# Loads of queries, keys, values and weight chunks in two or four transfers instead of one

## The chip, the core and the metric

The kernel runs on one core of a Trainium2 chip. The time is that of one launch in device microseconds (us); lower is better. The engines named below are PE (TensorE matmul), PEld (its weight load), DVE (VectorE), ACT (ScalarE), POOL (GpSimd) and SP (SyncE, which here only starts transfers). Transfers run on 16 DMA engines that all queues share.

## What is computed

Chunked softmax attention (8 batches, 8 heads, 576 rows, chunks of 64 rows) is followed by a mixture of eight experts with one expert per token. All 4608 tokens have 512 features.

```python
scores = scale * np.matmul(q_c, k_c.transpose(0, 1, 2, 4, 3))   # chunks of 64 x 64
attn = np.exp(scores - scores.max(-1, keepdims=True)); attn /= attn.sum(-1, keepdims=True) + 1e-09
x = np.matmul(attn, v_c)                                        # -> 4608 x 512
logits = x @ w_gate + modality_bias[modality_id]
e_idx = np.argmax(logits, axis=1)                               # gate_w: softmax weight of that expert
out[mask] = gate_w[mask, None] * (np.maximum(x[mask] @ w1[e], 0.0) @ w2[e])
```

## The kernel before

The attention goes in 18 rounds of 256 tokens. Round r needs one tile of queries and keys (`qk`, 128 partitions by 2048 numbers, 1024 KB) and one of values (`v`, 512 KB); three buffers each, so `load_qk(r + 3)` is called when the scores of round r are reduced, and `load_v(r + 3)` after the products with the values of round r. A round is `scores` (PE, L239), `differences` (DVE, L245 and L246), `exps` (ACT, L253), `halve` (POOL, L258), `transposes` (PE L291, copied by ACT L294), `values` (PE L306, copied by ACT L315), two `rows` (PE L324, DVE L326), `parts` (ACT L334) and `put`, which stores the round's 512 KB to DRAM (`xd`) from ACT's queue, L344. Round 0 has its own form, `opening` (L270), which computes heads 0 to 3 into one PSUM bank and heads 4 to 7 into another.

Rounds 0 to 7 run alone (the loop over `NPURE`). Rounds 8 to 17 are interleaved by `merge` with the experts' work: a `slot` is up to 384 tokens of one expert, gathered from `xd` by POOL (L756), and goes through eight chunks of 128 hidden features, each with 12 matmuls of `first` (L872) and up to 9 of `second` (L890). Chunks of weights are fetched in pairs (`fetch`, L819, 1024 KB, three buffers), split into two parts by ACT (`wh`, L830) and DVE (`wl`, L834). From slot 2 on a slot's tokens are also stored (`stash`) and read back in blocks (`place`). Thirteen slots run. After the eight pure rounds, `split` (PE L797, ACT L799, DVE L800) transposes the gathered tokens of slots 0 and 1. All orders are written out by hand; each engine runs its instructions in the order in which the program names them.

SP starts nearly all loads, in order. Round 9's queries and keys are loaded from ACT's queue instead (`load_qk(NPURE + 1, A)`, L1050), between the copies and the `parts` of round 7.

Each transfer that SP or ACT starts counts its landing on one of eight counters, DMAHW0 to DMAHW7, which are handed out in turn in the program's order of these transfers, those of both queues in one row. Before a transfer is started, its queue waits until the transfer that last had the same counter, the eighth before it, has landed. The queue's later instructions stand behind that wait: on ACT, its activations and copies too. POOL's transfers have counters of their own.

Of the kernel before, what the change touches and what calls it, by code (L numbers as in the profile page):

```python
# [18 lines left out]
B, H, S, D = 8, 8, 576, 64  # L19
P = 128  # L20
N = B * S
DM = H * D
# [46 lines left out]
NSPLIT = 2  # L69
# [26 lines left out]
def attention_moe(ctx: ExitStack, tc: tile.TileContext, qkv, mod, cst, bias, wcat, wfst, void, out):  # L96
    nc = tc.nc
    V, A, PE, G, SP = nc.vector, nc.scalar, nc.tensor, nc.gpsimd, nc.sync
# [14 lines left out]
    qks, vs, exs = {}, {}, {}  # L113
    st = {}

    def load_qk(r, eng=SP):
        if r < NT // 2 and r not in qks:
            qks[r] = ak.tile([P, 2, H, 2, 64], F32, name="qk", bufs=NB)
            eng.dma_start(qks[r].rearrange("p a h c s -> p (a h c s)"), qkv[r][:, 0:2 * 2 * DM])

    def load_v(r):
        if r < NT // 2:
            vs[r] = ak.tile([P, H, 2, D], F32, name="v", bufs=NB)
            SP.dma_start(vs[r].rearrange("p h c d -> p (h c d)"), qkv[r][:, 2 * 2 * DM:])

    cs = cp.tile([P, C_END], F32, name="cs")

    def consts(a, b):
        SP.dma_start(cs[:, a:b], cst[:, a:b])

    load_qk(0)
    consts(C_I, C_GW)
    load_qk(1)
    load_v(0)
    consts(C_GW, C_U)
    load_qk(2)
    load_v(1)
    consts(C_U, C_END)
    load_v(2)
    bs = cp.tile([P, 2, E], F32, name="bs")  # L140
    SP.dma_start(bs, bias)
# [668 lines left out]
    def expert(s):  # L810
        lv, k, _ = where(s)
        ereg[s] = SP.value_load(tabs[lv][0:1, k:k + 1], min_val=0, max_val=E - 1)

    def fetch(g, n=2):
        s, f = divmod(g, NF)
        if s not in ereg:
            expert(s)
        raw = rawr[g // 2 % 3][:, f % 2:f % 2 + n]
        SP.dma_start(raw, (wfst if s < NSPLIT else wcat)[ds(ereg[s], 1), :, f:f + n, :].rearrange("e p f c -> p (e f) c"))  # L819
        for i in range(n):  # L820
            raws[g + i] = raw[:, i]

# [24 lines left out]
    ereg = {}  # L847
# [62 lines left out]
    def slot(s):  # L910
# [5 lines left out]
        if s >= NSURE:  # L916
            expert(s)
            locate(s)
            for f in (0, 2, 4):
                fetch(s * NF + f)  # L920
            gather(s)
            stash(s)
            place(s)
            for f in range(AHEAD):
                wsplit(s * NF + f)
            for k in range(NK):
                turn(s, k)
                part(s, k)
        for f in range(NF):
            g = s * NF + f  # L930
            if s == 0:
                if f in FIRSTS:
                    fetch(FIRSTS[f])
            elif f % 2 == 0 and g + 6 < end:
                fetch(g + 6)
            h = first(xring[s % 2], W[g], g, nt * P)
            tick()
            if s < NSPLIT:
                advance((pooljobs,))
                advance((pooljobs,))  # L940
                wsplit(g + 2)
            else:
                advance()
                if s == NSPLIT and f == 0:
                    wsplit(g + 2)
                if g + AHEAD < end:
                    wsplit(g + AHEAD)
                advance()
            if pend is not None:
                second(ys, pend, W[g - 1], f - 1)  # L950
                tick()
            pend = h
            for c in PREP.get(s, REGULAR).get(f, ()) if s < NSURE else ():
                call(c, s if s > max(PREP) else 0)
            if s < NSPLIT:
                advance()
                advance()
            advance(pe=None if merging[0] else ts[1])
# [219 lines left out]
```

## Time and profile before

| | |
|---|---|
| runs | median 557.69 us of 3 (554.08 to 559.34) |
| profiled execution | 556.77 us by its own time, span 555.0 us |
| granted PE clock, mean | 0.989 |
| moved by DMA | 129.87 MB in 48626 packets, mean 234 GB/s |
| loads by SP | 17 of `qk`, 18 of `v`, 52 pairs of weight chunks; 1 of `qk` by ACT |

The profile page gives busy time and share of the span by engine; rows of the timeline read "start us, duration us, engine, line, operation, out<-in, count" and, in brackets, how long the engine had been idle and what ended it. ACTq and SPq are the instructions that these engines' sequencers handle themselves, here the starting of transfers. Rows of the windows view give busy time by engine in a stretch, then the granted clock, the DMA engines' busy share and GB/s. "us to landing" is the time from the start of a transfer's issue until it has landed; the profile has it for some transfers only.

### The profile page before, as it was taken

What the parts mean: (1) busy time and instruction counts of PE and PEld (TensorE: products, weight loads), DVE (VectorE), ACT (ScalarE), POOL (GpSimd) and SP (SyncE); (2) the same over time, 40 slices, a digit from 0 to 9 for tenths busy, and PEclk for the clock granted to TensorE, in tenths of its full rate; (3) what the DMA queues carried; (4) which work ended last, traced back from release to release, by engine and by line L of the source; (5) the groups of instructions that cost most, each with busy time, mean ns of one, the idle gap of its engine ahead of it and who ended that gap; (6) DMA issues with size and microseconds to landing.
All of it is one profiled execution on the core that took longest, in us unless ns stands there. A gap on an engine that the chain in (4) does not pass through costs nothing.

```text
span 555.0 us, 12219 instructions
## 1 busy us (share of the span) xinstructions
PE 525.4 (95%) x4933; PEld 474.2 (85%) x4933; DVE 359.5 (65%) x590; ACT 242.5 (44%) x403; POOL 163.9 (30%) x189
## 2 busy tenths in 40 slices
PE   7886997999999999999999999999999999999993
PEld 5875886988889899899999999999899999999992
DVE  4668786877686899656556465564656556466751
ACT  3453743555564443444434443443443434435530
POOL 3333455614356780340402205022040402202101
PEclk9999998999999999999999999999999999999997
DMA  8995897669766459597857668666685755557500
GB/s 341 411 363 190 303 410 271 220 209 411 272 235 196 155 153 351 201 309 213 276 175 230 243 209 254 194 217 199 224 280 163 267 165 205 192 188 237 184 20 27
DMA packets 48626, 129.87 MB, mean 234 GB/s; under 512 B 7100, under 2 KB 23852, under 8 KB 39600
## 3 DMA queue, kind: packets, MB, share of 16 engines
q1 hardware_dynamic: 36448, 99.34, 53.3%
q0 software_dynamic: 7072, 19.18, 9.9%
q10 hardware_dynamic: 5040, 10.49, 5.0%
q8 instruction: 40, 0.66, 0.5%
q14 instruction: 26, 0.21, 0.1%
HBM read 101.95 MB, written 27.83 MB: 234 GB/s over the span
## 4 chain that ended last, share of the span: by engine, by line
PE 72%; issue 14%; DVE 6%; DMA 3%; POOL 2%; ACT 1%; ACTq 0%; SPq 0%; POOLq 0%; DVEq 0%
PE y L872 26%; PE sb L890 20%; PE t L890 10%; PE y L324 5%; PE t L872 3%; PE y L306 2%; PE y L239 2%; PE t L291 1%; DMA xg<-xd,tk 1%; DMA qk<-in_qkv 1%; PE t L306 1%; PE sb L239 1%; POOL out L905 1%; DVE xr L326 1%; PE y L291 1%
## 5 line engine op out<-in xcount | busy, mean ns | idle before, releaser
L834 DVE TENSOR_TENSOR wl<-raw,wh 128x1024 fp32r<-128x1024 f32 x104 | 128.0, 1232 | 36.8 <-ACT wh L830 36.7
L880 ACT ACTIVATE hh<-y 128x384 fp32r<-128x384 f32 (+1 forms) x92 | 43.6, 474 | 179.6 <-PE y L872 179.4
L872 PE MATMUL y<-xh,wl 128*128 128x384 f32 (+1 forms) x368 | 120.7, 328 | 0.0
L872 PE MATMUL y<-xh,wh 128*128 128x384 f32 (+1 forms) x368 | 120.5, 327 | 0.0
L872 PE MATMUL y<-xl,wh 128*128 128x384 f32 (+1 forms) x368 | 120.1, 326 | 0.0
L881 DVE SCALAR_TENSOR_TENSOR hl<-y,hh 128x384 fp32r<-128x384 f32 (+1 forms) x92 | 49.1, 534 | 100.7 <-ACT hh L880 100.6
L830 ACT CAST wh<-raw 128x1024 fp32r<-128x1024 f32 x104 | 108.4, 1043 | 0.9 <-DMA raw<-in_wcat 0.9
L905 POOL DMA_INDIRECT out<-yo,tk x37 | 38.6, 1044 | 231.9 <-DVE yo L904 203.8
L890 PE MATMUL sb<-wh,hh 128*128 128x512 f32 x208 | 82.7, 397 | 0.0
L890 PE MATMUL sb<-wl,hh 128*128 128x512 f32 x208 | 81.9, 394 | 0.0
L890 PE MATMUL sb<-wh,hl 128*128 128x512 f32 x208 | 81.0, 389 | 0.0
L872 PEld LDWEIGHTS y<-xh,wh 128*128 128x128 f32 x368 | 69.2, 188 | 3.5
L872 PEld LDWEIGHTS y<-xl,wh 128*128 128x128 f32 x368 | 69.1, 188 | 3.2
L872 PEld LDWEIGHTS y<-xh,wl 128*128 128x128 f32 x368 | 69.1, 188 | 0.0
L756 POOL DMA_INDIRECT xg<-xd,tk x37 | 41.8, 1130 | 16.9 <-issue 8.7
L890 PEld LDWEIGHTS sb<-wh,hl 128*128 128x128 f32 x208 | 39.0, 188 | 8.8
L890 PEld LDWEIGHTS sb<-wh,hh 128*128 128x128 f32 x208 | 39.0, 188 | 6.2 <-issue 0.5
L540 POOL DMA_INDIRECT tab<-tg,pi x36 | 37.9, 1053 | 19.0 <-issue 13.3
L890 PEld LDWEIGHTS sb<-wl,hh 128*128 128x128 f32 x208 | 39.1, 188 | 4.5
L324 PE MATMUL y<-cs,xt 128*128 128x144 f32 x288 | 41.8, 293 | 1.1 <-DVE ex L246 0.8
L324 PEld LDWEIGHTS y<-cs,xt 128*128 128x128 f32 x288 | 38.5, 193 | 3.1 <-DVE ex L246 1.2
L258 POOL TENSOR_TENSOR sr<-ex 128x512 f32<-128x512 f32 x17 | 22.5, 1322 | 53.8 <-ACT ex L253 53.7
(234 smaller groups left out, 711.1 us busy)
## 6 DMA issues: line engine op xcount, KB each, us to landing
raw<-in_wcat SPq DMA_DIRECT2D x44, 1024.0 KB, 5.6
qk<-in_qkv SPq DMA_DIRECT2D x17, 1024.0 KB, 8.0
v<-in_qkv SPq DMA_DIRECT2D x18, 512.0 KB, 8.7
xd<-xr ACTq DMA_DIRECT2D x18, 512.0 KB, 5.2
raw<-in_wfst SPq DMA_DIRECT2D x8, 1024.0 KB, 4.9
xs<-xg SPq DMA_DIRECT2D x9, 768.0 KB, 7.7
xq<-xs SPq DMA_DIRECT2D x36, 192.0 KB, 3.8
qk<-in_qkv ACTq DMA_DIRECT2D x1, 1024.0 KB
```

Of the source, the lines that this page charges most:

```text
L239: PE.matmul(sp[c * 64:c * 64 + 64, u, h, :], b[us, 0, h, c], b[us, 1, h, c], start=True, stop=True)
L258: G.tensor_tensor(sring[r % 2][:, :, :, 0:32], exu[:, :, :, 0:32], exu[:, :, :, 32:64], ALU.add)
L324: PE.matmul(fp[:, p, 0:GWC], xt[:, p, :], gw[:, p, :], start=True, stop=True)
L540: w = G.indirect_dma_start(tab, bass.IndirectOffsetOnAxis(ap=pi[:, j:j + 1], axis=0), tg[:, j, :], None, bounds_check=E * CAP - 1, oob_is_ ...
L756: G.indirect_dma_start(xg[:, t, :], None, xd[0:n, :], bass.IndirectOffsetOnAxis(ap=tk[:, t:t + 1], axis=0), bounds_check=n - 1, oob_is_err ...
L830: A.copy(hi, raw)
L834: (G if pool else V).tensor_tensor(lo, raw, hi.bitcast(F32), ALU.subtract)
L872: PE.matmul(hp, a[:, ks], b[:, k, 0:n], start=(m == 0), stop=(m == 3 * NK - 1))
L880: A.activation(hh[:, 0:n], hp, AF.Relu)
L881: V.scalar_tensor_tensor(hl[:, 0:n], hp, 0.0, hh.bitcast(F32)[:, 0:n], ALU.max, ALU.subtract)
L890: PE.matmul(y, a[:, tsl], b[:, DM:2 * DM], start=(f == 0 and i == 0), stop=(f == NF - 1 and i == 2))
L905: w = G.indirect_dma_start(out, bass.IndirectOffsetOnAxis(ap=tk[:, t:t + 1], axis=0), yo, None, bounds_check=N - 1, oob_is_err=False)
```

## The change

A load of queries and keys becomes four transfers of 256 KB: queries and keys apart, heads 0 to 3 first, then heads 4 to 7. A load of values becomes two of 256 KB, by the same halves of the heads. A fetch of a pair of weight chunks becomes two transfers of 512 KB, one for each chunk. The bytes, buffers and places of the calls stay. The contiguous piece of a partition's row goes from 8 KB to 2 KB for queries and keys, from 4 KB to 2 KB for values, from 8 KB to 4 KB for weights.

```diff
     def load_qk(r, eng=SP):
         if r < NT // 2 and r not in qks:
             qks[r] = ak.tile([P, 2, H, 2, 64], F32, name="qk", bufs=NB)
-            eng.dma_start(qks[r].rearrange("p a h c s -> p (a h c s)"), qkv[r][:, 0:2 * 2 * DM])
+            src = qkv[r][:, 0:2 * 2 * DM].rearrange("p (a h c s) -> p a h c s", a=2, h=H, c=2)
+            for h in range(0, H, 4):
+                for a in range(2):
+                    eng.dma_start(qks[r][:, a, h:h + 4], src[:, a, h:h + 4])
...
-            SP.dma_start(vs[r].rearrange("p h c d -> p (h c d)"), qkv[r][:, 2 * 2 * DM:])
+            src = qkv[r][:, 2 * 2 * DM:].rearrange("p (h c d) -> p h c d", h=H, c=2)
+            for h in range(0, H, 4):
+                SP.dma_start(vs[r][:, h:h + 4], src[:, h:h + 4])
...
         raw = rawr[g // 2 % 3][:, f % 2:f % 2 + n]
-        SP.dma_start(raw, (wfst if s < NSPLIT else wcat)[ds(ereg[s], 1), :, f:f + n, :].rearrange("e p f c -> p (e f) c"))
+        for i in range(n):
+            SP.dma_start(raw[:, i:i + 1], (wfst if s < NSPLIT else wcat)[ds(ereg[s], 1), :, f + i:f + i + 1, :].rearrange("e p f c -> p (e f) c"))
```

What this does to the order of the queues is shown at three places. In the rows, `cs`, `bs` and `mid` are constants, and the names in brackets are the counters for which the instruction waits; lines of the changed kernel are 5 or 6 higher than those of the kernel before.

At the program's start, on SP. Before:

```order
L119 DMA qk<-in_qkv 128x2048
L129 DMA cs<-in_cst 128x128
L119 DMA qk<-in_qkv 128x2048
L124 DMA v<-in_qkv 128x1024
L129 DMA cs<-in_cst 128x576
L119 DMA qk<-in_qkv 128x2048
L124 DMA v<-in_qkv 128x1024
L129 DMA cs<-in_cst 128x596
L124 DMA v<-in_qkv 128x1024 [waits DMAHW0_49]
L141 DMA bs<-in_bias 128x16 [waits DMAHW1_49]
```

And after:

```order
L122 DMA qk<-in_qkv 128x512 x4
L134 DMA cs<-in_cst 128x128
L122 DMA qk<-in_qkv 128x512 x3
L122 DMA qk<-in_qkv 128x512 [waits DMAHW0_49]
L129 DMA v<-in_qkv 128x512 [waits DMAHW1_49]
L129 DMA v<-in_qkv 128x512 [waits DMAHW2_49]
L134 DMA cs<-in_cst 128x576 [waits DMAHW3_49]
L122 DMA qk<-in_qkv 128x512 [waits DMAHW4_49]
L122 DMA qk<-in_qkv 128x512 [waits DMAHW5_49]
```

The order of the bytes is the same, but the first eight transfers now hold a little less than two loads of queries and keys instead of three of them and two of values; from the ninth on SP waits. On PE, `opening` waits before for one transfer ahead of all its matmuls, after for the first two pieces ahead of heads 0 to 3 and for the other two ahead of heads 4 to 7; `scores` (L239) is divided in the same way.

At the end of round 7, on ACT, where round 9's queries and keys are loaded. Before:

```order
L315 COPY xt<-t_101 128x512 [waits PE_49]
L315 COPY xt<-t_102 128x512 [waits PE_49]
L119 DMA qk<-in_qkv 128x2048 [waits DMAHW1_49,DMAHW0_49]
L334 COPY lp_142<-y_98 128x64 [waits DVE_49]
L334 COPY lp_142<-y_99 128x64 [waits DVE_49]
L344 DMA xd<-xr 128x2x512
L799 CAST xh_164<-sb 128x768 [waits PE_49]
```

And after:

```order
L320 COPY xt<-t_113 128x512 [waits PE_49]
L320 COPY xt<-t_114 128x512 [waits PE_49]
L122 DMA qk<-in_qkv 128x512 [waits DMAHW3_49] x2
L122 DMA qk<-in_qkv 128x512 [waits DMAHW4_49]
L122 DMA qk<-in_qkv 128x512 [waits DMAHW6_49]
L339 COPY lp_154<-y_111 128x64 [waits DVE_49]
L339 COPY lp_154<-y_110 128x64 [waits DVE_49]
L349 DMA xd<-xr 128x2x512 [waits DMAHW7_49]
L804 CAST xh_176<-sb 128x768 [waits PE_49]
```

Counted back eight, the transfers waited for by ACT are: before, a store of round 3 and the first load of the program; after, the second half of round 9's values (the load of L124 issued at 59.62 us in the trace of before), the two halves of the fetch of chunks 2 and 3 (issued at 60.16 us), and, for the store (`put` of round 6), the first half of round 10's values (issued at 64.90 us).

In the interleaved part, on SP, around the loads of round 15's values and round 16's queries and keys (`tl` is a slot's list of tokens). Before:

```order
L819 DMA raw_113<-in_wfst 128x2048 [waits DVE_49]
L124 DMA v<-in_qkv 128x1024 [waits PE_49]
L119 DMA qk<-in_qkv 128x2048 [waits PE_49]
L604 TENSOR_LOAD e_tab_831
L604 ISA x2
L605 ISA
L605 DMA tl_168<-tab 128x3x16 [waits DMAHW4_49]
```

And after:

```order
L825 DMA raw_125<-in_wfst 128x1024 [waits DMAHW5_49,DVE_49]
L825 ISA
L825 DMA raw_125<-in_wfst 128x1024 [waits DMAHW6_49,DVE_49]
L129 DMA v<-in_qkv 128x512 [waits DMAHW7_49,PE_49]
L129 DMA v<-in_qkv 128x512 [waits DMAHW0_49]
L122 DMA qk<-in_qkv 128x512 [waits DMAHW1_49,PE_49]
L122 DMA qk<-in_qkv 128x512 [waits DMAHW2_49]
L122 DMA qk<-in_qkv 128x512 [waits DMAHW3_49]
L122 DMA qk<-in_qkv 128x512 [waits DMAHW4_49]
```

The eighth transfer after the first half of the values (its row waits for DMAHW7_49) is the store of round 12 (`put`, on ACT), which so waits for that half; in the trace of before this load is issued at 121.58 us, the store at 127.73 us. Before, the same store waits for the load of round 15's queries and keys, issued at 117.34 us.

## The prediction

> **What bounds the kernel now.** I read the page's busy times first, then the windows by stage, then PE's waits in the stages where PE isn't solid, and last the timeline around each wait that a transfer ends.
>
> ```profile
> span 555.0 us, 12219 instructions
> PE 525.4 (95%) x4933; PEld 474.2 (85%) x4933; DVE 359.5 (65%) x590; ACT 242.5 (44%) x403; POOL 163.9 (30%) x189
> ...
> 0.00:20.00 20.00, 16.49 (x349) 12.82 (x350) 9.51 (x18) 7.15 (x11) 6.13 (x21) 1.00 0.92 361
> 20.00:120.00 100.00, 85.94 (x1708) 77.40 (x1702) 78.78 (x147) 49.22 (x96) 44.91 (x52) 0.97 0.77 286
> 120.00:200.00 80.00, 77.05 (x1084) 69.33 (x1083) 60.67 (x116) 40.04 (x72) 42.20 (x46) 1.00 0.69 246
> 200.00:400.00 200.00, 200.00 (x1011) 182.15 (x1010) 125.07 (x191) 83.42 (x127) 44.12 (x45) 1.00 0.73 236
> ...
> SPq L819 <- DVE wl L834: 206.3, 39, 9.6
> ...
> PE y L270 <- DMA qk<-in_qkv: 1.4, 1, 1.4
> PE sb L239 <- DMA qk<-in_qkv: 0.7, 1, 0.7
> PE t L291 <- issue: 2.6, 1, 2.6
> PE y L797 <- ACT lp L334: 1.2, 1, 1.2
> PE y L797 <- DMA xg<-xd,tk: 1.7, 2, 1.1
> ```
>
> PE is the bound. From 200 to 400 us it is busy for all 200.00 us, so nothing that a weight fetch does earlier or later can show there, unless it comes too late. It won't: SP has the fetch waiting for a free buffer (DVE `wl`) for 206.3 us in total, and the chunk has the rest of its pair's time to land. The split of the fetches I therefore cost at 0; its cover is that wait. PE's idle time is in the first 200 us: 20 - 16.49 = 3.5, 100 - 85.94 = 14.1 and 80 - 77.05 = 3.0 us. That is the ceiling of any gain, and of it loads end only 1.4 + 0.7 us (the first two loads of queries and keys) and a gather 1.7 us. After 9 us PE waits for no load at all. So the change has little to win there, and the question is what it makes wait.
>
> **The start.** It wins at the first two loads.
>
> ```profile
> 0.76 0.40 SPq L119 DMA_DIRECT2D qk<-in_qkv  x1
> ...
> qk<-in_qkv SPq DMA_DIRECT2D x1, 1024.0 KB, 5.4
> ...
> 6.16 1.99 PE L270 MATMUL y<-qk 64*64 64x64 f32 x64 [1.36 <-DMA qk<-in_qkv]
> ...
> 8.83 1.99 PE L239 MATMUL sb<-qk 64*64 64x64 f32 x64 [0.69 <-DMA qk<-in_qkv]
> ...
> 10.75 1.97 PE L291 MATMUL t<-cs,ex 128*128 128x128 f32 x8
> ```
>
> The first load lands at 0.76 + 5.4 = 6.2 us, the second, 1024 KB and a 64 KB constant behind it, at 8.8: 2.67 us for 1088 KB, or 2.5 us for 1024 KB. Half a load lands 1.3 us before the whole. So half of `opening` runs before 6.2 us, and the scores of round 1 can run half before 8.83 us and end at 8.83 + 1.99 / 2 = 9.8 instead of 10.8 us. Transposes start then, if the exponentials, whose chain begins with the first half of `opening`, move by as much: -1.0 us. Bounds: 0, if the extra issues (0.40 us each, four where one was) or the wait from the ninth transfer on hold the stream up; -1.3 us, the whole half load. I take -1.0, since eight transfers hold nearly two loads, some 5 us of stream, and SP issues a piece in 0.40 us while it moves in 0.63.
>
> **SP's extra work.** It issues 3 x 17 + 18 + 52 = 121 transfers more, at about 0.4 us. In a round that is 4 more, 1.6 us. SP waits far longer than that, so 0.
>
> **ACT at the end of round 7.** Here ACT starts four transfers instead of one, and three of them, and the store behind them, wait for transfers that SP started late.
>
> ```profile
> 60.16 1.95 SPq L819 DMA_DIRECT2D raw<-in_wfst  x1
> ...
> 64.90 0.33 SPq L124 DMA_DIRECT2D v<-in_qkv  x1
> 64.97 0.38 ACTq L119 DMA_DIRECT2D qk<-in_qkv  x1
> ...
> 67.03 0.37 ACTq L344 DMA_DIRECT2D xd<-xr  x1
> 67.61 0.34 ACT L334 COPY lp<-y 128x64 f32<-128x64 f32 x2
> 67.81 0.84 ACT L799 CAST xh<-sb 128x768 fp32r<-128x768 f32 x1
> ...
> 69.49 0.43 PE L872 MATMUL t<-xh,wh 128*128 128x384 f32 x1
> ...
> v<-in_qkv SPq DMA_DIRECT2D x1, 512.0 KB, 8.7
> ...
> DMA to landing us min/median/max: 3.5/8.7/11.4
> ```
>
> Before, the load goes out at 64.97, the store at 67.03, and `xh` at 67.81 lets PE begin the first expert at 69.49 us. Now ACT's last piece waits for the fetch issued at 60.16, which can't land after the values behind it in the same queue, and the store waits for the first half of the values issued at 64.90. The whole of them landed 8.7 us later, at 73.6; the shortest landing of any such load is 3.5 us, which would be 68.4. The half is ahead of its other half and of nothing else, so I put it between, at 70.5. Then the store issues at 70.5, and `xh` starts 0.3 us later, at 70.8 instead of 67.81: +3.0 us, with bounds 68.7 - 67.8 = +0.9 and 73.9 - 67.8 = +6.1. Behind the store stand `xh`, `hh` and the copies of the next transposes; PE waits for `xh` already (it waited 1.2 us for `lp` there), so all of it is on the path. What is late next is SP, whose later pieces wait in turn for this store; the loads behind it are for rounds 10 and 11, two rounds off.
>
> **ACT at the store of round 12.** The same thing, in the interleaved part.
>
> ```profile
> 118.89 0.34 SPq L732 DMA_DIRECT2D tl<-tab  x1
> ...
> 121.58 0.34 SPq L124 DMA_DIRECT2D v<-in_qkv  x1
> ...
> 124.04 0.41 SPq L605 DMA_DIRECT2D tl<-tab  x1
> ...
> tl<-tab SPq DMA_DIRECT2D x1, 24.0 KB, 9.6
> ...
> tl<-tab SPq DMA_DIRECT2D x1, 24.0 KB, 13.4
> ...
> 127.73 0.37 ACTq L344 DMA_DIRECT2D xd<-xr  x1
> 128.71 1.07 ACT L294 COPY at<-y 128x512 f32<-128x512 f32 x2 [1.04 <-PE y L291]
> ...
> 129.60 1.16 PE L306 MATMUL y<-at,v 64*64 64x64 f32 x64
> ...
> 132.21 7.91 DMA xg<-xd,tk
> ```
>
> The store now waits for the first half of the values issued at 121.58. Their landing isn't in the profile, but the lists of tokens ahead of and behind them in the queue landed at 118.89 + 9.6 = 128.5 and 124.04 + 13.4 = 137.4. Between lie 1024 KB of weights, 512 KB of values and 1024 KB of queries and keys, and the half is done after 1280 of these 2560 KB: midway, 133.0; at the start's 2.5 us for 1024 KB, 128.5 + 3.1 = 131.6. I take 132.2, nearer the second, since the store itself and the gather that shared the engines then are held back or not yet out. ACT is free at 132.2 + 0.4, and the copies `at` that stood at 128.71 run 3.9 us later; PE had 129.60 - 128.71 = 0.9 us of work in between, of which about half the copy's 1.07 must be over, so PE stands some 3.5 us. Bounds: +0.5 (landing at 128.5) and +5 (133.5).
>
> PE's wait for the gather then goes. The third gather landed at 132.21 + 7.91 = 140.1 and PE had waited 1.7 us; it is issued by POOL after the list has landed and doesn't depend on PE there, so PE, 3.5 us late, finds it landed: -1.7 us. The next store (round 13) waits for the first half of round 16's values in the same way; by then ACT and PE are late by more than that wait, 0.
>
> **Shares of the engines.** Transfers of different queues take turns packet by packet:
>
> ```profile
> q1 hardware_dynamic: 314, 2.19, 66.8%
> q10 hardware_dynamic: 310, 1.05, 33.6%
> ...
> q10 hardware_dynamic: 5040, 10.49, 5.0%
> ```
>
> From 70 to 78 us, with both queues full, SP's queue q1 moved 314 packets and ACT's q10 310. Loads of 2 KB rows so give stores and gathers a larger part, and the gather of 7.9 us shortens too, which the term above already holds. The Trainium skill's page "DMA: Bandwidth & Descriptors", section "Queues, rings and completion order", says that each engine goes round robin between queues by packets; the trace agrees, with 314 beside 310. The rate of 2 KB packets is ACT's own: 10.49 MB in 5.0% of 16 x 555 us is 23.6 GB/s for each engine, q1 in the window above 2.19 MB in 66.8% of 16 x 8 us, 25.6. So a load would move up to 8% slower. After the start that is 0, since no load ended a wait of PE there, though values took up to 11.4 us to land; at the start it is at worst 8% of 2.5 us, +0.2.
>
> **The sum.** -1.0 + 0 + 3.0 + 3.5 - 1.7 = +3.8 us on the profiled execution's own 556.77 us: 560.6. The median of the runs is 557.69, 0.9 above it, so runs of the changed kernel should lie around 561.
>
> **Rivals.** *The counters don't bite.* The waits on ACT end before ACT gets there, because eight small transfers are a shorter queue than eight large ones and land sooner. Point of decision: the halves land within 2.1 us (64.90 to 67.03) and 6.2 us (121.58 to 127.73) of their issue. Then -1.0 and -1.7 stay, and perhaps the 2.6 us that PE stood for its instructions while the engines were full: 551.5 to 554, faster. Against it: the shortest landing of values is 3.5 us and the median 8.7. 0.2.
>
> *Every store waits.* There are 18 stores on ACT, and where the engines are full (share 0.77 from 20 to 120 us) each may stand for its eighth predecessor as these two do. With three or four more places at 3 us: 560.6 + 9 to 12, 570 to 573. Against it: the other stores' predecessors are loads issued a round or more before them, and values land in 8.7 us by the median. 0.15.
>
> *Nothing on the path changes.* PE is solid from 200 us, the start's gain is eaten by issue time and the ACT waits fall into ACT's idle 56%: 556 to 558. Against it: ACT is waited for at 67.9 us. 0.2.
>
> *The fixed part of a transfer comes into the path.* If transfers went one after another, each of the 121 more would add about the 3.5 us of the shortest landing of 256 or 512 KB: far over 100 us. Against it: landings of 8.7 us with new loads issued every 6 us or less show that they overlap. 0.02. The same page, section "Rules for kernel authors", speaks for this rival: it wants transfers of at least 1 MiB and many small ones joined into one. The section "Anatomy of one DMA" fits a fixed 2.0 us for each transfer that POOL issues; 121 of them in a row would be 242 us, an estimate from that page.
>
> **Chances.** The forecast (558.5 to 563.5) has 0.43. Within 1% of 557.69, which is about what a measurement of this kernel can tell from no change, is 552.1 to 563.3. Faster than that: about half of the first rival, 0.11, and a little for what I don't see, 0.13. Slower: all of the second and fourth, 0.17, and the upper bounds of the two ACT waits (6.1 + 5 instead of 3.0 + 3.5 makes 565.2), 0.13: 0.30. Same: 0.57. The range leaves out the fourth and the far part of the second rival, and the lower end of the first: 552 to 569.
>
> **What would show it.** In the new profile: PE's first matmuls of L275 near 4.9 us and transposes near 9.8; a hole of PE and ACT after 65 us that ends with the store (L349) near 70.5, the first `xh` after it and the experts' first matmul 3 us later; ACT standing before the store of round 12 while `v` is in flight; no PE wait for `xg` near 140 us; 200 us of solid PE in the middle. I am wrong if the stores' issues keep their distance to the copies before them, if PE waits for `qk` or `v` after 10 us, or if PE isn't solid from 200 us on.

## The result, and the profile after

The changed kernel took 563.32 us (median of 6 runs, 561.52 to 566.68), the kernel before 557.9 us in the same comparison. The ratio is 1.010, with a 95% interval of 1.0057 to 1.0143: some 5.4 us slower, a loss of one per cent that is clear of zero by its interval. The profiled execution took 563.22 us, its span is 561.4 us, 6.4 more than before.

Stores are numbered below by the round whose tokens they hold, from 0: store 6 is the one that ACT starts at the end of round 7, between `lp` and `xh`. Where an expectation speaks of the store of round 7, or at the end of it, this one is meant.

The page of the kernel after, its span and busy times:

```profile
span 561.4 us, 12573 instructions
...
PE 527.6 (94%) x4933; PEld 476.9 (85%) x4933; DVE 358.3 (64%) x590; ACT 242.0 (43%) x403; POOL 164.2 (29%) x189
```

And the windows by stage, up to 400 us (busy time of PE, PEld, DVE, ACT, POOL with counts, then granted clock, DMA share, GB/s):

```profile
0.00:20.00 20.00, 15.10 (x347) 11.31 (x347) 9.88 (x18) 7.60 (x11) 6.13 (x21) 0.83 0.91 321
20.00:120.00 100.00, 85.50 (x1683) 77.68 (x1683) 75.10 (x143) 47.71 (x92) 43.88 (x52) 0.93 0.82 286
120.00:200.00 80.00, 74.55 (x1071) 67.59 (x1070) 56.58 (x107) 37.73 (x70) 38.22 (x42) 0.98 0.75 251
200.00:400.00 200.00, 200.00 (x1010) 182.14 (x1009) 126.42 (x199) 83.46 (x128) 49.14 (x50) 1.00 0.73 235
```

The middle is as solid as it was, PE 200.00 of 200 us. What is lost is lost before 200 us. At the top of PE's waits in the kernel after stand two rows that end with ACT: the one for `lp` was 1.2 us before, and all waits for `at` together 0.3. The row for `xg`, the gather, is gone. Two of these rows, and that for the first load:

```profile
PE y L802 <- ACT lp L339: 4.6, 1, 4.6
PE y L311 <- ACT at L299: 3.7, 1, 3.7
...
PE y L275 <- DMA qk<-in_qkv: 1.8, 1, 1.8
```

ACT's timeline around the first of them, store 6 (ACTq rows are transfers being started; their second number is how long the starts took, standing included):

```profile
64.63 1.09 ACTq L122 DMA_DIRECT2D qk<-in_qkv  x2
...
67.95 2.68 ACTq L122 DMA_DIRECT2D qk<-in_qkv  x2
70.67 0.33 ACT L339 COPY lp<-y 128x64 f32<-128x64 f32 x2 [3.24 <-DMA raw<-in_wfst]
71.64 0.38 ACTq L349 DMA_DIRECT2D xd<-xr  x1
72.07 0.80 ACT L804 CAST xh<-sb 128x768 fp32r<-128x768 f32 x1 [1.07 <-PE y L802]
```

ACT stands twice in a row there: with its own last two pieces of `qk` until the weight chunk has landed at 70.6 us, then another 0.6 us with the store, until 71.64 (67.03 before). PE waits for the `lp` that stands behind the first of the two, and for nothing behind the store. From PE's timeline, after and then before:

```profile
70.94 1.54 PE L802 MATMUL y<-cs,xg 128*128 128x128 f32 x6 [4.58 <-ACT lp L339]
72.28 2.12 PE L329 MATMUL y<-cs,xt 128*128 128x144 f32 x8
74.03 0.69 PE L878 MATMUL t<-xh,wh 128*128 128x384 f32 x1
...
77.08 1.14 PE L329 MATMUL y<-cs,xt 128*128 128x144 f32 x8
```

```profile
67.89 0.88 PE L797 MATMUL y<-cs,xg 128*128 128x128 f32 x6 [1.24 <-ACT lp L334]
68.60 1.15 PE L324 MATMUL y<-cs,xt 128*128 128x144 f32 x8
69.49 0.43 PE L872 MATMUL t<-xh,wh 128*128 128x384 f32 x1
...
71.75 1.14 PE L324 MATMUL y<-cs,xt 128*128 128x144 f32 x8
```

The wait costs more than its length. From the first to the last of these rows PE does the same work in both kernels without a pause, but it takes 77.08 - 70.94 = 6.14 us after and 71.75 - 67.89 = 3.86 before. The granted clock differs (windows of after, then of before):

```profile
71.00:74.00 3.00, 3.00 (x14) 3.00 (x15) 1.10 (x2) 1.50 (x2) 0.00 (x0) 0.50 1.03 406
74.00:77.00 3.00, 3.00 (x14) 3.00 (x14) 2.28 (x4) 0.00 (x0) 0.00 (x0) 0.69 1.04 403
```

```profile
67.89:71.75 3.86, 3.86 (x26) 3.81 (x27) 3.64 (x6) 1.57 (x3) 0.00 (x0) 1.00 1.01 408
```

So 3.3 us more of waiting (4.58 for 1.24) and 2.3 us of slower matmuls behind it make up nearly all of the 5.7 us by which store 7 is later, counted from store 5. The experts' first matmul moves from 69.49 to 74.03 us.

That chunk isn't late: SP started it at 61.16 us (60.16 before), and it lands 8.6 us after its start. SP stands too, but with the next pair; its timeline has 4.62 us for two starts, of which 3.8 are a wait for a store by the row of SP's waits:

```profile
65.85 4.62 SPq L825 DMA_DIRECT2D raw<-in_wfst  x2
```

ACT's timeline around the second place, store 12:

```profile
130.20 0.21 ACT L339 COPY lp<-y 128x64 f32<-128x64 f32 x1 [0.47 <-DVE xr L331]
135.04 0.37 ACTq L349 DMA_DIRECT2D xd<-xr  x1
135.50 1.07 ACT L299 COPY at<-y 128x512 f32<-128x512 f32 x2 [5.09 <-DMA v<-in_qkv]
```

ACT is through with `lp` at 130.41 us and starts the store 4.63 us later, when the first half of the values has landed; the copies `at`, for which PE waits, stand behind it. PE then stands 3.73 us, and here too the granted clock is low behind the wait: 0.63 from 136.14 to 140.74 us. The work from there to the end of the next `rows` takes 7.62 us, 6.28 before.

The distance from one store to another shows what each place cost. From store 5 to store 9 it was 37.60 us before and is 41.07 after (+3.5; it had been +5.7 at store 7, and 2.2 came back). From store 11 to store 14 it was 32.82 and is 36.06 (+3.2, with the gather's wait already taken back). The second of these is again wait and clock: 3.7 + 1.3 - 1.7 for the gather. Store 2 stood 3.02 us and store 3 1.03, and nothing of that is left at store 5, which is 0.3 us earlier than before. Stretch by stretch, to store 5, 9, 11, 14 and 17: -0.3 + 3.5 - 0.4 + 3.2 + 0.6 = 6.6 us.

### The profile page after: what moved, and what is told of

Same layout as the page of the kernel before. It is cut to its first block, busy times and chain, and to the rows that moved or that the text cites. A ratio compares the mean times of both kernels' runs of the same rounds, so it can differ in the third digit from the quotient of the medians.

```text
span 561.4 us, 12573 instructions
## 1 busy us (share of the span) xinstructions
PE 527.6 (94%) x4933; PEld 476.9 (85%) x4933; DVE 358.3 (64%) x590; ACT 242.0 (43%) x403; POOL 164.2 (29%) x189
## 4 chain that ended last, share of the span: by engine, by line
PE 73%; issue 14%; DVE 4%; DMA 4%; POOL 2%; ACT 1%; SPq 1%; ACTq 0%; POOLq 0%; DVEq 0%
PE y L878 26%; PE sb L896 20%; PE t L896 10%; PE y L329 5%; PE t L878 4%; PE y L244 2%; PE y L311 2%; DMA raw<-in_wfst 2%; PE t L311 1%; PE y L296 1%; POOL out L911 1%; DMA v<-in_qkv 1%; PE t L296 1%; PE sb L244 1%; DMA qk<-in_qkv 1%
## 5 line engine op out<-in xcount | busy, mean ns | idle before, releaser
L329 PE MATMUL y<-cs,xt 128*128 128x144 f32 x288 | 43.4, 301 | 2.7 <-issue 2.0
L329 PEld LDWEIGHTS y<-cs,xt 128*128 128x128 f32 x288 | 39.8, 199 | 4.5 <-issue 2.2
```

Source lines behind the costliest of these rows:

```text
L329: PE.matmul(fp[:, p, 0:GWC], xt[:, p, :], gw[:, p, :], start=True, stop=True)
```

## The experiments

In the three groups of runs that follow the kernel before took 591 to 593 us, not 558. No trace of it was kept there. In that of the weights alone, a kernel of the same time (1.0012), PE waited 12.0 us for what the rows call "issue" at the products with the values (1.4 before), ACT had one wait of 9.9 us for "remote", and the mean granted clock was 0.961 (0.989 before). Why this was so isn't known. So a kernel is compared with the kernel before of its own group, by the ratio with its 95% interval, and places are compared by distances between stores.

### Only the counters

Large loads stay whole; transfers of 4 bytes take the counters that the pieces would take.

```diff
+    def beat(n, eng):
+        for _ in range(n):
+            eng.dma_start(ticks[:, nt[0]:nt[0] + 1], qkv[0][0:1, 0:1])
+            nt[0] += 1
...
+            beat(3, eng)      # behind a load of queries and keys
+            beat(1, SP)       # behind a load of values
+        beat(n - 1, SP)       # behind a pair of weight chunks
```

> The kernel before with its large loads whole, and behind each of them, in the same queue, as many transfers of 4 bytes as the change adds (three behind queries and keys, one behind values, one behind a pair of weight chunks). The output is the same. Theory (the completion counters, which eight hardware transfers share in turn, make ACT stand in front of its store): the store of round 7 now waits for the whole of the values issued at 64.9 us, which landed at 73.6 in the profile before, so ACT stands there some 5 to 6 us; at the store of round 12 the eighth transfer before lies just behind queries and keys that were issued before 118.9, so it stands 0 to 1.5 us; no gain at the start. In all 562 to 565 us against 557.7. Rival 1 (rows of 2 KB and smaller transfers move slower or disturb the others): large rows are back, so 557 to 558.5, and no hole before the store of round 7. Rival 2 (SP's issue time): the 121 issues are there as well, so 561 to 564, but with SP late at its fetches and no hole of ACT at the store.

Measured: 605.37 us, ratio 1.0193 (1.0159 to 1.0227). The counters alone, with the rows as large as before, cost as much as the change and more. ACT's timeline shows store 6 standing for the whole load of values:

```profile
76.44 0.50 ACT L344 COPY lp<-y 128x64 f32<-128x64 f32 x2 [0.73 <-DMA ticks<-in_qkv]
79.62 0.39 ACTq L354 DMA_DIRECT2D xd<-xr  x1
80.06 0.80 ACT L809 CAST xh<-sb 128x768 fp32r<-128x768 f32 x1 [3.11 <-DMA v<-in_qkv]
```

It stood 2.68 us, less than the 5 to 6 that I expected, since ACT was already late: SP stood for the counters as well, a weight chunk came late, and ACT waited 6.91 us for it at 61.6 us. That is why the total is above the 562 to 565 us (1.008 to 1.013) that the theory gave. By rival 1 (rows) there should have been no loss, so it falls as the only cause; that SP's standing costs something in this kernel is seen. SP's issue time (rival 2) is here as well and isn't ruled out by this run.

### Whole loads near the stores

Everything in pieces as after, but a few loads whole, so that the eighth transfer before some stores is an old one. Here near stores 6, 12 and 13:

```diff
+            if r in (9, 16, 17):     # load_qk: one transfer
+                eng.dma_start(qks[r].rearrange("p a h c s -> p (a h c s)"), qkv[r][:, 0:2 * 2 * DM])
+                return
...
+            if r in (10, 15, 16):    # load_v: one transfer
...
+        m = n if g in (4, 10, 12) else 1    # fetch: one transfer for the pair
```

> The kernel after, with the split taken back for 3 loads of queries and keys (rounds 9, 16, 17), 3 of values (10, 15, 16) and 3 pairs of weight chunks, so that the eighth transfer before the stores of rounds 7, 12 and 13 is an old one; about 9 of the 60 loads of the first 200 us are whole, the rest is in pieces as in after. Theory (counters): the holes of ACT at the stores of rounds 7 and 12 go, what the start wins stays, the wait for the gather near 140 us (1.7 us) comes back: 556 to 558 us. Rivals (size of rows and transfers, or SP's issue time): most of both is still there, so 561 to 563 us, as after.

Measured: 600.58 us, ratio 1.0115 (1.0074 to 1.0156). By the total the theory failed here and the rivals held. The timeline says why: stores 6, 12 and 13 no longer stand, but the next one, store 7, does.

```profile
77.39 0.25 ACT L448 ACTIVATE va<-lg 128x56 f32<-128x56 f32 x1
81.75 0.37 ACTq L355 DMA_DIRECT2D xd<-xr  x1
82.22 1.07 ACT L305 COPY at<-y 128x512 f32<-128x512 f32 x2 [4.58 <-DMA qk<-in_qkv]
```

It stood 4.11 us, for a piece of round 10's queries and keys. In the kernel after it hadn't, because ACT came there late. A wait had hidden behind a wait; a cure has to cover both.

### Rows of 2 KB, one transfer

```diff
-            eng.dma_start(qks[r].rearrange("p a h c s -> p (a h c s)"), qkv[r][:, 0:2 * 2 * DM])
+            t = ak.tile([P, 4, 520], F32, name="qk", bufs=NB)     # 512 numbers, 8 of padding
+            eng.dma_start(t[:, :, 0:512], qkv[r][:, 0:2 * 2 * DM].rearrange("p (g x) -> p g x", g=4))
```

Values likewise, as two rows of 512.

> The kernel before with the same number of transfers, but the tiles of queries and keys and of values padded behind every 512 numbers, so that each of these loads is one transfer that moves rows of 2 KB, as the pieces of the change do. Theory (counters): same time as before, 557 to 558.5 us, perhaps 1 us less where the gather and the stores get a larger share of the engines. Rival 1 (size of rows): what the change costs behind the start is here too, 561 to 564 us.

Measured: 594.84 us, ratio 1.0032 (1.0004 to 1.0059). A small loss: about a third of the change's, and no store stands more than 0.84 us. It lies in part at the start, where PE waits for loads; from the windows of this kernel, and of the one with only the weights split, whose first loads are whole, the stretches 0 to 3, 3 to 6 and 6 to 9 us:

```profile
0.00:3.00 3.00, 1.80 (x5) 0.70 (x6) 0.76 (x7) 1.28 (x1) 2.35 (x13) 1.00 0.33 59
3.00:6.00 3.00, 1.40 (x5) 0.33 (x3) 0.00 (x0) 0.00 (x0) 1.23 (x7) 1.00 1.04 388
6.00:9.00 3.00, 1.49 (x64) 1.30 (x64) 1.57 (x3) 0.15 (x1) 0.00 (x0) 0.71 1.05 388
```

```profile
0.00:3.00 3.00, 1.80 (x5) 0.70 (x6) 0.76 (x7) 1.28 (x1) 2.35 (x13) 1.00 0.42 93
3.00:6.00 3.00, 1.80 (x5) 0.34 (x3) 0.00 (x0) 0.00 (x0) 1.23 (x7) 1.00 1.00 388
6.00:9.00 3.00, 2.29 (x76) 2.10 (x80) 1.75 (x3) 0.34 (x1) 0.00 (x0) 1.00 0.98 411
```

The last numbers are GB/s: 59 against 93 at first, the same 388 from 3 to 6 us, 388 against 411 from 6 to 9. The first matmul on queries and keys is at 6.63 us here and at 6.02 there: 0.6 us for rows of 2 KB in one transfer.

### The start alone

```diff
+            if r < 2:     # four transfers as in the change, else one
```

> The kernel before, with only the first two loads of queries and keys (rounds 0 and 1) as four transfers each. The stores' eighth transfers before are the same as in before. The prediction's term for the start: -1.0 us, 556.7 us (bounds 556.4 to 557.7). Against it stands the profile after, where rounds 1 to 8 are only 0.1 to 0.8 us earlier: 557.0 to 557.6. Transposes of round 1 near 9.8 us by the term, near 10.7 by the other.

Measured: 592.92 us, ratio 1.0007 (0.9976 to 1.0037). No gain can be seen. Transposes of round 1 start at 10.98 us, so the -1.0 us isn't there: the first half of a load is early (first matmul at 4.72 us), the second half is later than the whole load was (6.65 us against 6.02 to 6.16), and the next load behind it too. (The profiled execution of this kernel took 599.53 us, 6.6 more than the median; the kernel after shows the same at its start, below.)

### The kernel after, beside the next three

> The kernel after once more, beside the experiments of this group, so that they are compared under the same conditions. As in the first comparison: ratio to before near 1.010, with ACT standing before the stores of rounds 2, 6 (as the store's own number counts from 0: the store at the end of round 7 of the loop) and 12.

Measured: 596.63 us, ratio 1.0105 (1.0065 to 1.0145). Store 2 stands 2.28 us, ACT's last two pieces 2.31 us and the store behind them 0.62, store 12 3.83 us. The change costs the same here as in the first comparison.

### No young transfer before any store

The edit of the second experiment with `r in (6, 9, 10, 11, 16, 17)`, `r in (5, 10, 15, 16)` and `g in (4, 10, 12)`.

> The kernel after, with six loads of queries and keys (rounds 6, 9, 10, 11, 16, 17), four of values (5, 10, 15, 16) and three pairs of weight chunks whole again, chosen so that the eighth hardware transfer before every store is an old one. All other loads and 49 of the 52 pairs stay in pieces, the first two loads too. In the kernel with fewer whole loads (near the stores of rounds 7, 12, 13) the wait had moved to the next store, which stood 4.11 us. Theory (counters at the stores): no store stands more than 1 us, and the time is that of before, ratio 0.997 to 1.003. Rivals (size of rows and transfers; SP's issue time): about three quarters of both is still there, ratio 1.007 to 1.011, as after.

Measured: 591.24 us, ratio 1.001 (0.9975 to 1.0045). The loss is gone, with 12 of the 18 loads of queries and keys, 14 of the 18 of values and 49 of the 52 pairs of chunks still in pieces: 36 + 14 + 49 = 99 of the 124 additional transfers. No store stands. The same place as above, ACT's timeline around store 6:

```profile
68.85 0.38 ACTq L120 DMA_DIRECT2D qk<-in_qkv  x1
...
70.89 0.37 ACTq L355 DMA_DIRECT2D xd<-xr  x1
70.99 0.59 ACT L326 COPY xt<-t 128x512 f32<-128x512 f32 x1
71.47 0.34 ACT L345 COPY lp<-y 128x64 f32<-128x64 f32 x2
71.67 0.85 ACT L810 CAST xh<-sb 128x768 fp32r<-128x768 f32 x1
```

The store starts between two copies without a gap. Rows and SP's issues, four fifths of which are still there, were to give 1.007 to 1.011; both fall as main causes. The whole loads spare SP some of its waits near these places, too, so this run alone doesn't part ACT's standing from SP's.

### One part alone

Queries and keys in four transfers, the rest as before:

> Only the loads of queries and keys in four transfers; values and weights as before. The store of round 7's end now has the whole pair of weight chunks issued at 60.16 us as its eighth transfer before, and one of ACT's pieces the values of the round before. Theory (counters): ACT stands 2 to 4 us there; at the store of round 12 the eighth before is a pair of weight chunks that was issued behind the list of tokens of 118.89 us, so 0 to 3 us; the gather's wait takes up to 1.7 back: ratio 1.002 to 1.009. Rival 1 (rows): two thirds of the pieces' rows are here, 1.005 to 1.008 with no store standing.

Measured: 598.29 us, ratio 1.0139 (1.0094 to 1.0184): all of the loss, and over the range that I gave. ACT needs 1.04 us to start its last two pieces before store 6, store 7 stands 1.36 us, store 12 3.63, and between stores 7 and 8 ACT waits once more, 4.78 us, for what the row calls "remote", which the counters don't explain.

Pairs of weight chunks in two transfers, the rest as before:

> Only the pairs of weight chunks in two transfers, 52 issues more on SP, 24 to 40 of them in the stretch that PE fills. Theory (counters): every store's eighth transfer before is old (values a round and a half back, or a store), except that of round 13, a list of tokens issued at 124.04: 0 to 0.5 us. Ratio 0.998 to 1.002. Rival 2 (SP's issue time, 0.4 us each): 1.002 to 1.006.

Measured: 591.09 us, ratio 1.0012 (0.9975 to 1.0049), and no store stands over 0.4 us. 52 of the additional transfers cost nothing that can be measured.

### Each of the prediction's two terms by itself

The edit of the second experiment twice: once with only the loads near stores 12 and 13 whole, so that the places up to round 8 are left as in after, and once the other way round.

```diff
-            if r in (9, 16, 17):   ...   (10, 15, 16)   ...   (4, 10, 12)
+            if r in (16, 17):      ...   (15, 16)       ...   (10, 12)       # waits to round 8 are left
+            if r in (6, 9, 10, 11):...   (5, 10)        ...   (4,)           # waits of stores 12, 13 are left
```

With the waits up to round 8 left:

> The kernel after with only the loads near the stores of rounds 12 and 13 whole again (queries and keys of 16 and 17, values of 15 and 16, two pairs of weight chunks): stores 2, 6 and 7 keep their young eighth transfer, 12 and 13 have an old one. It is the prediction's term for the end of round 7 (+3.0 us) by itself; after's own trace had experts' first matmul 4.5 us later there, of which some 2 came back by 98 us. Ratio by the term 1.004 (with nothing won at the start 1.005); by after's trace 1.004 to 1.009; store 12 doesn't stand, the wait for the gather comes back.

With those of stores 12 and 13 left:

> The counterpart: the loads near the stores of rounds 2, 6 and 7 whole (queries and keys of 6, 9, 10, 11, values of 5 and 10, one pair of weight chunks), those near the stores 12 and 13 in pieces. The prediction's terms +3.5 - 1.7 = +1.8 us by themselves, and nothing at the start: ratio 1.003; by after's trace (4.6 stood, 2.1 came back) 1.002 to 1.006. Store 12 stands 3.5 to 5 us, no store before it. If both this and its counterpart come out at 1.000 to 1.002, the loss of after isn't a sum over places.

Measured: with the waits up to round 8, 599.82 us, ratio 1.0118 (1.0082 to 1.0154), above both numbers expected. With those of stores 12 and 13, 590.8 us, ratio 0.9975 (0.9945 to 1.0004): no loss, though the wait is there, as ACT's timeline of that kernel shows:

```profile
132.81 0.21 ACT L345 COPY lp<-y 128x64 f32<-128x64 f32 x1 [0.47 <-DVE xr L337]
136.60 0.37 ACTq L355 DMA_DIRECT2D xd<-xr  x1
137.07 1.07 ACT L305 COPY at<-y 128x512 f32<-128x512 f32 x2 [4.04 <-DMA v<-in_qkv]
```

Store 12 stood 3.58 us, and PE waited 2.7 us for `at`. From store 11 to store 14 it took 34.93 us, in kernels of these groups whose store 12 stands 0.84 us or not at all 34.2 to 37.0. In the first pair of profiles the same stretch went from 32.82 to 36.06. So in these groups the stretch was as long without the wait. In the trace of the weights alone another loss stands in its place: the products with the values behind store 12, 1.16 us in before, lie from 137.23 to 141.20 us with waits for "issue" between them, and the granted clock is 0.50 from 141 to 147 us. In the kernel whose store 12 stands these products run through, in 1.99 us, at a clock of 0.51 for 3 us. Why the one loss comes where the other doesn't wasn't tried.

The distances from store 5 to store 7 put all of this in one table:

| kernel | store 5 to 7, us | store 5 to 9, us | ratio |
|---|---|---|---|
| before (first comparison) | 13.06 | 37.60 | 1 |
| after (first comparison) | 18.76 | 41.07 | 1.010 |
| after again | 18.14 | 42.44 | 1.0105 |
| waits to round 8 left | 18.21 | 42.56 | 1.0118 |
| whole near stores 6, 12, 13 | 18.45 | 46.87 | 1.0115 |
| queries and keys alone in pieces | 16.11 | 43.84 | 1.0139 |
| counters alone | 20.14 | 43.19 | 1.0193 |
| rows of 2 KB | 13.02 | 37.13 | 1.0032 |
| start alone | 13.06 | 39.35 | 1.0007 |
| no young transfer | 13.04 | 36.50 | 1.001 |
| weights alone split | 13.03 | 36.97 | 1.0012 |
| waits of stores 12, 13 left | 13.02 | 36.47 | 0.9975 |

Every kernel of the table that is 1% slower has 3 to 7 us more between stores 5 and 7, and none of the others has any of it. Up to store 9 it is some 5.5 to 6 us for after, measured against the last two rows: 1.0% of 592 us. The two kernels below aren't in the table: in one the stores don't run on ACT, so their distances don't show where ACT and PE are, and the other changes the order of the matmuls.

### Stores from POOL

```diff
-        A.dma_start(xd[2 * r * P:(2 * r + 2) * P, :].rearrange("(u p) c -> p u c", p=P),
+        G.dma_start(xd[2 * r * P:(2 * r + 2) * P, :].rearrange("(u p) c -> p u c", p=P),
...
-            load_qk(NPURE + 1, A)
+            load_qk(NPURE + 1)
```

> The kernel after with all its pieces, but the 18 stores issued by POOL, whose transfers have counters of their own, and the load of round 9 by SP instead of ACT; the eight counters are as crowded by SP's loads as in after. Theory (it costs because ACT, which PE waits for, stands): ACT never stands for a transfer, ratio 0.997 to 1.004, unless POOL, which issues in order and takes about 1 us for an issue, is late at the gathers because it stands for a store's data. Rivals (size of rows; SP's issue time; SP's own standing for the counters): as after, 1.008 to 1.012.

Measured: 583.06 us, ratio 0.9833 (0.9803 to 0.9863): faster than both kernels, and by more than the theory gave. ACT starts no transfer and `lp` runs straight into `xh`. PE waits 1.2 us for `lp` and 0.4 for `at`; in the first comparison it was 1.2 and 0.3 before, 4.6 and 3.7 + 1.4 after. But the gain over the kernel before isn't that. Its profile is level with the others up to the 15th `hh` on ACT (220.3 us; after again 222.1, weights alone 218.8), 6 to 9 us ahead at the 16th (224.4 against 233.8 and 230.5), and stays ahead. In between the others have one long wait of ACT; from the timelines of the weights alone, and of this kernel:

```profile
230.53 0.49 ACT L881 ACTIVATE hh<-y 128x384 fp32r<-128x384 f32 x1 [9.93 <-remote]
```

```profile
224.42 0.49 ACT L886 ACTIVATE hh<-y 128x384 fp32r<-128x384 f32 x1 [2.33 <-PE y L878]
...
230.19 0.69 ACT L908 ACTIVATE yo<-sb,tl 128x512 f32<-128x512 f32 x1 [3.93 <-issue]
```

ACT's wait of 9.93 us, which no row explains and which the kernel before didn't have in its own profile (its longest for an `hh` was 2.9 us), is not here; two of 5.3 us stand earlier, at 105 and 197 us. So the gain over before hangs on where that wait falls. What this run adds on the change is less: with all the pieces, and SP's counters as crowded, PE's two waits for ACT are gone. That nothing else of the loss is left isn't shown, since the total has the missing wait in it: at the 15th `hh` this kernel was 1.5 us behind the weights alone and 1.8 ahead of after again. Whether it wins anything where the kernel before takes 558 us wasn't tried.

### The start by partitions

```diff
-            eng.dma_start(qks[r].rearrange("p a h c s -> p (a h c s)"), qkv[r][:, 0:2 * 2 * DM])
+            n = P // 2 if r < 2 else P
+            for u in range(0, P, n):
+                eng.dma_start(qks[r][u:u + n].rearrange("p a h c s -> p (a h c s)"), qkv[r][u:u + n, 0:2 * 2 * DM])
...
-        for h in range(H):
-            for u in range(2):
+        for u in range(2):
+            for h in range(H):
```

The new order of the matmuls stands in `opening` and in `scores`, so it holds for all 18 rounds, not for two as the expectation says.

> The kernel before, with the first two loads as two transfers of 64 partitions each, so that rows stay 8 KB, and the matmuls of these two rounds in an order that uses the first 64 partitions first. Theory (pieces win at the start what their rows of 2 KB give back): here nothing is given back, the first matmul is at 4.9 to 5.2 us, the second half of load 0 is there when the whole was, and the transposes of round 1 start 0.5 to 1.0 us before those of the kernel before (10.75 us in its profile): ratio 0.997 to 1.001. Rival: 64 partitions keep only a part of the engines busy, then the second half is later and nothing or less than nothing is won, 1.000 to 1.004.

Measured: 605.15 us, ratio 1.0205 (1.017 to 1.0239). The theory and the order of the matmuls both went wrong, and a cause could be seen for each. A transfer of 64 partitions moved at about half the rate with the engines as busy (windows of this kernel, then of the kernel before; DMA share and GB/s last):

```profile
3.00:6.00 3.00, 1.79 (x5) 0.33 (x3) 0.00 (x0) 0.00 (x0) 1.23 (x7) 1.00 0.99 232
6.00:9.00 3.00, 2.18 (x36) 2.00 (x38) 0.00 (x0) 0.00 (x0) 0.00 (x0) 1.00 1.06 194
```

```profile
3.00:6.00 3.00, 1.80 (x5) 0.33 (x3) 0.00 (x0) 0.00 (x0) 1.25 (x7) 1.00 1.01 407
6.00:9.00 3.00, 2.16 (x70) 1.97 (x73) 1.61 (x3) 0.20 (x1) 0.00 (x0) 1.00 0.98 408
```

Half a load lands when a whole one did (first matmul at 6.10 us), the second half one load later (8.79 us). The Trainium skill's page "DMA: Bandwidth & Descriptors", section "Rules for kernel authors", advises against two transfers to halves of the partitions, since they share the engines and go one after the other; the trace agrees, and here they lost rate too, 232 GB/s against 407. The matmuls of `scores` took longer in the new order, 1.91 us a round against 1.16 where PE isn't held up (timelines of this kernel and of before):

```profile
27.82 1.91 PE L241 MATMUL sb<-qk 64*64 64x64 f32 x64
```

```profile
28.68 1.16 PE L239 MATMUL sb<-qk 64*64 64x64 f32 x64
```

The rows of PE's groups add up to 20.7 + 17.7 + 3.9 = 42.3 us for all 18 rounds, against 11.8 + 11.4 + 2.0 = 25.2 before.

## Why the prediction was right, by its own steps

The time, 563.3 for 561, and the mechanism were right in the main: loads in pieces make the eighth transfer before a start on ACT a young one, ACT stands for it, and PE for ACT. All three places came out dearer than forecast (-0.3 us for -1.0, +3.5 for +3.0, +3.2 for +1.8, by the distances of the stores), and the time lies just under the upper end of the range. That it is as near as it is was partly luck: the sum holds neither the 2.3 and 1.3 us that PE lost at the lower clock behind its two waits nor the 2.2 us that came back by store 9.

**The start, -1.0 us: fell.** The first matmul came earlier than I said, 4.49 us for 4.9, but transposes at 10.73 for 10.75 before. The exponentials of `opening` did end 1.0 us earlier (9.77 for 10.75). What failed is that the scores of round 1 would end at 9.8: they began at 8.44 for 8.83, took 2.37 us for 1.99 at a granted clock of 0.50 (1.00 before) and ended at 10.8. In the start alone, the scores' second half waited 0.38 us for its load, too. I also let the second half of the load land when the whole had, and gave smaller rows 0.2 us at worst. The second half's matmuls started at 6.94 instead of 6.16 us: from 3 to 6 and from 6 to 9 us the pieces moved at 306 and 364 GB/s, the whole loads at 407 and 408, with the engines 0.97 to 1.01 busy. The kernel with only this part in it gained nothing (1.0007).

**SP's issues and the split of the fetches, 0: held** (1.0012 for the fetches alone). What I gave no price is that SP stands for the counters too, as in the 4.62 us for two chunks. For the chunk that held ACT at the end of round 7 it makes little difference, since it was started only 1.0 us later than before; the values for which store 12 stood were started late.

**ACT at the end of round 7, +3.0 us: the right place, by another row.** I had ACT's last piece land no later than the store's wait, held only the store to count, at 70.5 us, and let PE wait for `xh` behind it; the wait of 1.2 us from which I took this is for `lp`, and PE waits for `xh` in neither trace. In the trace the chunk let ACT go at 70.6, and PE, which needs `lp`, went on at 70.94 for 67.89: 3.05 us, the size forecast, but for the wait of ACT's own pieces. The store followed at 71.64 and held nobody up. What the term lacked is the slower work behind the wait: the experts' first matmul is 4.5 us later and store 7 5.7. The slower work is seen in other kernels too: in the 3 us behind PE's waits of 3.65 us (after again) and 4.23 us (waits to round 8 left) the granted clock was 0.50 and 0.52, behind those of 1.2 to 1.5 us at the same place (before, no young transfer, waits of stores 12 and 13 left) it was 1.00. The term also lacked the 2.2 us that came back by store 9. By the runs the waits up to round 8 are the whole loss where the kernel before takes 592 us: 1.0118 with them alone, 0.9975 to 1.0032 in the five kernels of the table without them.

**ACT at store 12, +3.5, and the gather's wait, -1.7: right in the first profile, too small by the clock, and not seen in the later groups.** The wait was 4.63 us, PE's part 3.7. The store came at 135.04 for 132.2, because SP started the values at 128.44 for 121.58, 6.9 us later, where store 11 was only 2.8 later. The gather's row is gone: +3.2 from store 11 to 14 in place of +1.8, of which 1.3 is PE's work at the lower clock. In the later groups the same wait cost nothing on balance.

**The rivals.** "The counters don't bite" falls: four stores stood. "Every store waits" falls as well, but nearer than I thought: stores 2 and 3 stood, and were absorbed, and store 7 was kept from it only by ACT's delay. "Nothing on the path changes" falls with PE's two waits for ACT. The fixed part of a transfer is out: 52 more of them cost nothing that can be measured, and 99 more don't either (1.001, 0.9975 to 1.0045).

**Open:** why the loss with queries and keys alone (1.0139) isn't smaller than with all parts (the intervals overlap); what the waits called "remote" are, on which the gain of the kernel with POOL's stores hangs; how much SP's late start of the values adds to the wait at store 12; and how much of store 12's wait would cost where the kernel before takes 558 us, by itself.

## What to carry to other kernels

Here a transfer cost more than its bytes and its issue: it took one of eight counters, and the next transfer to need that counter made its engine stand. Before splitting loads in such a program, count back the eighth transfer before each one that a computing engine starts, its loads as well as its stores, and see whether it has landed by then. Price a wait of PE with the slower work behind it: here 4.6 us of waiting was followed by another 2.3 us lost. Split only where someone waits for the first half, keep the loads before such a transfer whole, or start it from an engine for which nobody waits; and look for the second wait behind the first before judging a cure.

## What the runs showed of the hardware that wasn't expected

Behind PE's waits for ACT of 2.7 to 4.6 us the granted clock was 0.50 to 0.63 for the next 3 to 5 us, and PE took, in one place, 6.14 us for work of 3.86; behind waits of 1.2 to 1.5 us it was 1.00. One load in rows of 2 KB moved at 59, 388 and 388 GB/s from 0 to 3, 3 to 6 and 6 to 9 us, one in rows of 8 KB at 93, 388 and 411; the change's pieces of 256 KB moved at 91, 306 and 364, where the kernel before had 85, 407 and 408. From 3 us on the engines were about as busy in all of them, 0.97 to 1.05. Transfers to 64 partitions moved at 232 and 194 GB/s where whole ones had 407 and 408. Of 64 matmuls of 64x64, taking the upper and lower partitions in alternation took 1.16 us, one half after the other 1.91 us, at a granted clock of 1.00 in both.
